# Moving a 2 KB input load from the ScalarE queue to the SyncE queue, behind the first weight load, in a one-core decode kernel

## The chip, the cores and the metric

The kernel runs on one core of one Trainium2 chip. The metric is the device time of one execution in microseconds (us). A profiled execution also gives a span, from its first to its last instruction, which is about 1.3 us shorter than the time. Kernels are compared only within the same rounds.

Names used below: PE is TensorE, DVE is VectorE, ACT is ScalarE, POOL is GpSimd, SP is SyncE. "SPq" and "ACTq" are the instruction sequencers of SP and ACT when they issue a DMA. There are 16 DMA engines; each works off packets from queues: q1 holds what SP issues, q10 what ACT issues.

## The reference, cut to what matters

One token (x of 1024 values) goes through a layer norm and then two branches that are added: a grouped-query attention over a cache of 65,536 positions with 4 key/value heads, and a small MLP block.

```python
x = A_x                                        # 1 x 1 x 1024, bf16: 2 KB
xn = _layernorm(x)
# attention: q = xn @ wq (8 MB); scores with k_cache (64 MB); softmax; times v_cache (64 MB); @ wo (8 MB)
# MLP: two layers of 1024 x 1024 (2 MB each), w3 1024 x 3584 and w4 3584 x 1024 (7 MB each)
return x + _A_ref(xn, A_k_cache, A_v_cache, A_wq, A_wo) + _B_ref(xn, B_w1, B_w2, B_w3, B_w4)
```

With one token, every byte of weights and cache is used once. About 170 MB must be read, whatever the kernel does.

## The kernel before

All large loads are issued by SP and land in one buffer with three slots of 8 MB, `KV[:, 0..2]`. Slot 0 takes wq, slot 1 takes w1 and w2, slot 2 takes w3. After that the slots take the cache blocks: K0 in slot 0, V0 in slot 1, K1 in slot 2, and so on. A slot is reloaded when the work that reads it is done.

```python
def kv_load(s, ch, src, n, bufs=None):
    _dma(q_sp, chan(ch), lambda e: e.dma_start(out=KV[:, s, 0:n], in_=src), writes=b_KV[s] if bufs is None else bufs)

_dma(q_act, chan("x"), lambda e: e.dma_start(out=x_bf, in_=A_x[0, 0, :].rearrange("(p j) -> p j", p=P)), writes=[b_x])
kv_load(0, "s0", rows_src(A_wq, 0, 8), 8 * HQD)
kv_load(1, "w1", rows_src(B_w1, 0, 8), 8 * D, b_w1)
_dma(q_sp, chan("w2"), lambda e: e.dma_start(out=KV[:, 1, 8 * D:16 * D], in_=rows_src(B_w2, 0, 8)), writes=b_w2)
kv_load(2, "s2", rows_src(B_w3, 0, 8), 8 * F)
# ... constants on POOL ...
_op(q_dve, lambda e: e.tensor_copy(xT, x_bf), reads=[b_x], writes=[b_xT])      # first DVE instruction
layer_norm(xT, b_xT, xn, xn_bf, b_xn, 200)
# ... query projection on PE: reads slot 0 and xn ...
issue(3)          # K0 into slot 0
# ... second layer norm, w1 layer, gelu, w2 layer ...
issue(4)          # V0 into slot 1
# ... third layer norm, w3 layer, gelu ...
issue(5)          # K1 into slot 2; then the cache blocks, each of which issues two more loads when it is done
```

When the program is put together, the first DMA of SP and the first of ACT are moved ahead of the start barrier, so that they go out at once. Everything else of SP's list follows the barrier.

```python
heads = {e: next(i for i in code if i.opcode == "Drain" and i.engine == e) for e in (nc.sync.engine, nc.scalar.engine)}
# ...
for eng in (nc.sync.engine, nc.scalar.engine):
    first = next(i for i in code[n_before:] if i.engine == eng)
    assert first.opcode == "DMACopy" and not first.sync_info.on_wait
    code.remove(first)
    code.insert(code.index(heads[eng]), first)
```

## Time and profile before

| | before |
|---|---|
| time, median of 3 | 400.42 us (400.32 to 400.59) |
| span of the profiled run | 399.1 us |
| data read | 169.97 MB, mean 426 GB/s |
| busy share of the span: DVE, PE, ACT | 55%, 42%, 6% |
| share of all 16 DMA engines' span taken by q1 | 98.7% |

These lines are from the profile's page of the kernel before. The first is the mean busy share of the 16 DMA engines in 40 equal slices of the span (9 is 90% or more). The two queue lines give packets, MB and the share of 16 engines' span. The last is the chain of waits that ended last, by line.

```profile
DMA  9999899999999999999999999999999999999995
...
DMA packets 3759, 169.97 MB, mean 426 GB/s; under 512 B 548, under 2 KB 552, under 8 KB 808
...
q1 hardware_dynamic: 3608, 169.87, 98.7%
...
q10 hardware_dynamic: 144, 0.00, 0.0%
...
DMA KV<-in_A_k_cache_dram 45%; DVE KV L460 18%; DMA KV<-in_B_w_dram 8%; DMA KV<-in_A_x_dram 6%; PE S_ps L411 3%; PE OT_ps L518 2%; DVE mrow L481 2%; PE M_ps L426 2%; PE S_ps L474 2%; PE S_ps L379 1%; ACT p_sb L496 1%; DVE Yall L395 1%; DVE pT_f L509 1%; DVE pT_f L419 1%; PE PT_ps L505 0%
```

The DMA engines hardly ever rest: the time seems to be set by the stream of loads. No compute engine is above 55%. Note also the 6% that the chain gives to the load of x. That figure looks like a prize of 22 us.

The next lines are from the timeline of the kernel before (those of SPq as the view of SP alone has them): start in us, duration in us, engine, line, operation, out<-in, and in brackets the idle time before it with what ended it.

```profile
0.00 0.39 SPq L290 DMA_DIRECT2D KV<-in_A_wq_dram  x1
0.12 0.37 ACTq L295 DMA_DIRECT2D KV<-in_A_x_dram  x1
...
22.24 0.17 DVE L339 CAST KV<-KV 128x8 f32<-128x8 bf16 x1 [22.24 <-DMA KV<-in_A_x_dram]
...
27.53 4.98 PE L379 MATMUL S_ps<-KV 128*32 128x512 bf16 x64 [1.36 <-DVE KV L359]
...
32.58 0.33 SPq L290 DMA_DIRECT2D KV<-in_A_k_cache_dram  x1
51.26 0.33 SPq L290 DMA_DIRECT2D KV<-in_A_v_cache_dram  x1
...
69.25 0.19 DVE L439 TENSOR_TENSOR gh_bf<-KV 128x28 bf16<-128x28 f32 x1
...
69.47 0.33 SPq L290 DMA_DIRECT2D KV<-in_A_k_cache_dram  x1
...
69.50 8.77 DVE L460 STREAM_TRANSPOSE KV<-KV 128x4096 f32<-128x4096 f32 x2
...
99.84 0.33 SPq L290 DMA_DIRECT2D KV<-in_A_v_cache_dram  x1
100.21 0.43 SPq L290 DMA_DIRECT2D KV<-in_A_k_cache_dram  x1
```

x is issued at 0.12 us and is 2 KB, yet DVE waits for it until 22.24 us. The query projection starts at 27.53 us, K0 is issued at 32.58, V0 at 51.26, K1 at 69.47 us. The first cache block (its first work is DVE L460) starts at 69.50 us, when two things are there: the output of the gelu behind w3 (DVE L439, the last work of the MLP before the cache; w4 comes at the very end), and K0, which lands at 69.48 us.

The trace's packet records show why x is late. On each engine they alternate (the records do not name the engine; a share is put together from packets that start as another ends): a 65,536 B packet of wq from q1 (2.418 us), a 16 B packet of x from q10 (0.009 us), eight times over. The Trainium skill's page "DMA: Bandwidth & Descriptors", section "Queues, rings and completion order", describes this round-robin between queue rows at packet granularity, and this trace agrees: x's packets start 2.42 us apart from 4.1 to 21.6 us. The turn here is per packet and not per byte, so the small load ends with the large one.

### The profile page before, as it was taken

To read this page: it belongs to the slowest core of one execution; us is meant where nothing else is said; L and a number is where in the kernel's file an instruction comes from. 1 tells how busy PE (TensorE), PEld (TensorE's weight loads), DVE (VectorE), ACT (ScalarE), POOL (GpSimd) and SP (SyncE) were. 2 spreads that over 40 slices of the span, in tenths; PEclk is the share of its full clock that TensorE was granted. 3 is DMA by queue.
4 is the path that set the end of the run, shared out by engine and by line. 5 is a ranking of instruction groups with operands and counts; after the bars stand their busy time and mean duration, and the time that the engine had idled before them with its cause. 6 is when DMAs were issued, how large, how long until landed. Compare 5 with 4: busy or idle time off the path is not lost.

```text
span 399.1 us, 3429 instructions
## 1 busy us (share of the span) xinstructions
PE 168.9 (42%) x1523; PEld 59.0 (15%) x1484; DVE 221.4 (55%) x260; ACT 23.9 (6%) x50; POOL 7.7 (2%) x31
## 2 busy tenths in 40 slices
PE   0034767338033713460357036413541362137394
PEld 0011334012001210110012001101120110012232
DVE  0024222994298549833984597269647952895201
ACT  1000000011001100110011002000100110011000
POOL 5000000000000000000000000000000000000000
PEclk9998568555655665575557555855585558555969
DMA  9999899999999999999999999999999999999995
GB/s 420 420 388 493 383 441 466 447 415 427 420 427 429 434 460 434 434 427 420 434 427 420 466 440 434 421 420 434 427 427 466 434 440 420 420 427 434 418 414 229
DMA packets 3759, 169.97 MB, mean 426 GB/s; under 512 B 548, under 2 KB 552, under 8 KB 808
## 3 DMA queue, kind: packets, MB, share of 16 engines
q1 hardware_dynamic: 3608, 169.87, 98.7%
q8 instruction: 5, 0.08, 0.1%
q10 hardware_dynamic: 144, 0.00, 0.0%
q14 instruction: 2, 0.02, 0.0%
HBM read 169.87 MB, written 0.00 MB: 426 GB/s over the span
## 4 chain that ended last, share of the span: by engine, by line
DMA 59%; DVE 25%; PE 12%; issue 1%; ACT 1%; SPq 1%; POOL 0%
DMA KV<-in_A_k_cache_dram 45%; DVE KV L460 18%; DMA KV<-in_B_w_dram 8%; DMA KV<-in_A_x_dram 6%; PE S_ps L411 3%; PE OT_ps L518 2%; DVE mrow L481 2%; PE M_ps L426 2%; PE S_ps L474 2%; PE S_ps L379 1%; ACT p_sb L496 1%; DVE Yall L395 1%; DVE pT_f L509 1%; DVE pT_f L419 1%; PE PT_ps L505 0%
## 5 line engine op out<-in xcount | busy, mean ns | idle before, releaser
L460 DVE STREAM_TRANSPOSE KV<-KV 128x4096 f32<-128x4096 f32 x32 | 140.3, 4422 | 44.3 <-DMA KV<-in_A_k_cache_dram 44.3
L474 PE MATMUL S_ps<-KV,Ycur 128*32 128x512 bf16 x512 | 60.7, 624 | 132.5 <-DVE KV L460 132.5
L518 PE MATMUL OT_ps<-KV,pT_f 128*32 128x512 bf16 x512 | 47.2, 511 | 4.0 <-issue 3.0
L474 PEld LDWEIGHTS S_ps<-KV,Ycur 128*32 128x32 bf16 x512 | 14.3, 126 | 160.0 <-DVE KV L460 142.4
L496 ACT ACTIVATE p_sb<-S_ps,brun 128x1024 bf16<-128x1024 f32 x16 | 17.8, 1114 | 276.6 <-DVE brun L494 176.1
L509 DVE STREAM_TRANSPOSE pT_f<-PT_ps 128x512 f32<-128x512 f32 x32 | 22.5, 702 | 14.0 <-PE PT_ps L505 14.0
L481 DVE TENSOR_REDUCE mrow<-S_ps 128x1 f32<-128x1024 f32 x16 | 19.3, 1205 | 11.3 <-PE S_ps L474 11.3
L484 PE MATMUL M_ps<-Rm,Lmat 128*128 128x16 bf16 x16 | 3.1, 194 | 38.0 <-DVE Rm L482 38.0
L529 DVE SCALAR_TENSOR_TENSOR O_acc<-O_acc,ff,OT_ps 128x512 f32<-128x512 f32 x12 | 9.0, 748 | 14.7 <-PE OT_ps L518 14.7
L518 PEld LDWEIGHTS OT_ps<-KV,pT_f 128*32 128x32 bf16 x512 | 13.1, 115 | 23.8 <-issue 16.4
L411 PE MATMUL S_ps<-KV 128*32 128x512 bf16 x88 | 12.1, 538 | 2.7 <-DVE KV L359 2.7
L339 DVE CAST KV<-KV 128x8 f32<-128x8 bf16 x1 | 0.2, 172 | 22.2 <-DMA KV<-in_A_x_dram 22.2
L578 PE MATMUL S_ps<-KV,o_bf 128*1 128x512 bf16 x64 | 9.9, 484 | 4.5 <-DMA KV<-in_A_wo_dram 4.5
L505 PE MATMUL PT_ps<-p_sb,permR 128*128 128x512 bf16 x16 | 9.7, 607 | 0.8
L426 PE MATMUL M_ps<-ident_f,pT_f 64*128 64x2 f32 (+2 forms) x32 | 7.9, 373 | 2.5 <-DVE pT_f L419 2.5
L484 PEld LDWEIGHTS M_ps<-Rm,Lmat 128*128 128x128 bf16 x16 | 1.7, 104 | 49.3 <-DVE Rm L482 49.3
L582 DVE COPY pT_f<-S_ps 1x512 f32<-1x512 f32 x1 | 0.7, 679 | 14.4 <-PE S_ps L578 14.4
L426 PEld LDWEIGHTS M_ps<-ident_f,pT_f 64*128 64x128 f32 (+2 forms) x32 | 7.7, 326 | 4.7 <-DVE pT_f L419 3.1
L419 DVE COPY pT_f<-S_ps 64x512 f32<-64x512 f32 (+1 forms) x3 | 2.1, 685 | 10.8 <-PE S_ps L411 10.8
L505 PEld LDWEIGHTS PT_ps<-p_sb,permR 128*128 128x128 bf16 x32 | 3.3, 102 | 27.5 <-ACT p_sb L496 14.7
L364 PE MATMUL M_ps<-KV 8*128 8x8 bf16 x1 | 0.2, 184 | 16.1 <-DVE Dmat_f L363 16.1
L642 POOL MEMSET pT_f<- 64x512 f32 x1 | 0.5, 520 | 312.4 <-PE OT_ps L518 312.4
(88 smaller groups left out, 90.2 us busy)
## 6 DMA issues: line engine op xcount, KB each, us to landing
KV<-in_B_w_dram SPq DMA_DIRECT2D x1, 7168.0 KB, 48.0
KV<-in_B_w_dram SPq DMA_DIRECT2D x1, 4352.0 KB, 27.4
KV<-in_B_w_dram SPq DMA_DIRECT2D x2, 2048.0 KB, 28.3
KV<-in_B_w_dram SPq DMA_DIRECT2D x1, 1792.0 KB, 31.3
KV<-in_B_w_dram SPq DMA_DIRECT2D x1, 768.0 KB, 32.7
KV<-in_B_w_dram SPq DMA_DIRECT2D x1, 256.0 KB, 32.9
KV<-in_A_k_cache_dram SPq DMA_DIRECT2D x8, 46.7
KV<-in_A_v_cache_dram SPq DMA_DIRECT2D x8, 28.1
```

What stands on the lines that cost most here:

```text
L411: fns.append(lambda e, j=j, k=k, mv=mv: e.matmul(S_ps[32 * (k % 4):32 * (k % 4) + 32, bank + k // 4, :], vec[:, j:j + 1].broadcast_to([P, ...
L419: _op(q_dve, lambda e, b=b, nb=nb: e.tensor_copy(pT_f[0:32 * nb, b, :], S_ps[0:32 * nb, bank + b, :]), reads=[b_S[bank + b]], writes=[b_pT ...
L426: fns.append(lambda e, b=b, nb=nb, c=c: e.matmul(M_ps[:, c0 + 16 * b + c:c0 + 16 * b + 4 * nb:4], pT_f[0:32 * nb, b, c:512:4], ident_f[0:3 ...
L460: _op(q_dve, lambda e: e.transpose(out=KV32[:, s, o:o + 4096], in_=KV32[:, s, o:o + 4096]), reads=[b_KV[s][sub]], writes=[b_KV[s][sub]], l ...
L474: fns.append(lambda e, we=we, cm=cm, mv=mv: e.matmul(S_ps[32 * cm:32 * cm + 32, n % 4, :], Ycur[:, we, :, :].rearrange("p a g -> p (a g)") ...
L481: _op(q_dve, lambda e: e.reduce_max(mrow[:, k:k + 1], S_ps[:, 2 * k:2 * k + 2, :].rearrange("p b c -> p (b c)"), axis=AX.X), reads=b_S[2 * ...
L496: _op(q_act, lambda e: e.activation(p_sb[:, :, :].rearrange("p b c -> p (b c)"), S_ps[:, 2 * k:2 * k + 2, :].rearrange("p b c -> p (b c)") ...
L505: _op(q_pe, lambda e: e.matmul(PT_ps[:, :], permR[:, :], p_sb[:, n % 2, :], start=True, stop=True), reads=[b_p[n % 2], b_const], writes=[b ...
L509: _op(q_dve, lambda e: e.transpose(out=pT_f[:, n % 2, :], in_=PT_ps[:, :]), reads=[b_PT], writes=[b_pT[n % 2]], loop=True)
L518: fns.append(lambda e, q=q, q4=q4: e.matmul(OT_ps[32 * q4:32 * q4 + 32, g % 2, :], pT_bf[:, n % 2, q, :, 1], KV[:, s, 8192 * sub + 512 * q ...
L529: _op(q_dve, lambda e: e.scalar_tensor_tensor(out=O_acc[:, 0:512], in0=O_acc[:, 0:512], scalar=ff[:, k:k + 1], in1=OT_ps[:, k, :], op0=ALU ...
L578: _grp(q_pe, [lambda e, j=j, jj=jj: e.matmul(S_ps[32 * jj:32 * jj + 1, 1, :], o_bf[:, j:j + 1], KV[:, 0, j * D + 512 * jj:j * D + 512 * (j ...
```

## The change

The load of x is issued by SP, directly behind wq. ACT has no DMA any more, so only SP's first DMA (wq) is moved ahead of the barrier. One may hope that ACT's start is relieved, that wq no longer shares its engines with x, and that x arrives as wq does, in time for the projection that needs both.

```diff
-        _dma(q_act, chan("x"), lambda e: e.dma_start(out=x_bf, in_=A_x[0, 0, :].rearrange("(p j) -> p j", p=P)), writes=[b_x])
         kv_load(0, "s0", rows_src(A_wq, 0, 8), 8 * HQD)
+        _dma(q_sp, chan("x"), lambda e: e.dma_start(out=x_bf, in_=A_x[0, 0, :].rearrange("(p j) -> p j", p=P)), writes=[b_x])
...
-        heads = {... for e in (nc.sync.engine, nc.scalar.engine)}
+        heads = {... for e in (nc.sync.engine,)}
...
-        for eng in (nc.sync.engine, nc.scalar.engine):
+        for eng in (nc.sync.engine,):
```

## The prediction

> **What bounds the kernel.** The stream of weight and cache loads on the SyncE queue. The profile's page gives 169.97 MB at a mean of 426 GB/s; SyncE's queue (q1) takes 98.7% of all 16 DMA engines' span. The trace's packet records show 64 KB packets back to back at 2.418 us each (16 x 65,536 B / 2.418 us = 434 GB/s). Unused engine time sums to about 5.4 us: 1.2 us before the first packets, 3.9 us in the last 10 us, only about 0.25 us between. So only what delays or lengthens this stream moves the time.
>
> **What x does now.** The ScalarE queue issues x at 0.12 us, yet the timeline's first DVE instruction (the cast of x) waits until 22.24 us, for x. x is only 2 KB; it is late because of sharing. In the packet records each engine alternates: one 65,536 B packet of wq on q1, one 16 B packet of x on q10, eight times, from 4.1 to 21.6 us. The Trainium skill ("DMA: Bandwidth & Descriptors", section "Queues, rings and completion order") describes this round-robin by packet; the trace agrees. x's last completion is at 22.21 us, wq's at 22.02 us. Issuing x from another queue thus buys no early x.
>
> **What the change removes, adds, moves.** It takes a 0.37 us DMA issue from ScalarE's start and adds about 0.4 us to SyncE's, between wq and w1. w1 goes out near 1.3 us in place of 0.92 us: harmless, wq keeps the engines until 21 us. x's eight 16 B packets and its completion now stand behind wq's eight packets in the same ring. Each takes 0.009 us in the records, so about 0.08 us per engine, the same work in another place. wq should finish about 0.07 us earlier, x at about 22.1 to 22.5 us.
>
> **How much is critical.** The chain x, layer norm, query projection (27.53 to 32.58 us) frees slot 0, and the first K load is issued at 32.58 us. But it queues behind w1, w2 and w3, which occupy the engines until about 48 us: some 15 us of slack. The V load is issued at 51.26 us, while K keeps the engines until 67 us; the next K load at 69.47 us, with V keeping them until 86 us. A shift of x by a few us is swallowed. The end (w4, last rows, output) only follows the stream. The chain of waits lists the x load with 5.5%, but in those 22 us the wq load is needed by the same projection and lands at the same time, so that share cannot be won.
>
> **Predicted:** 400.4 us, range 399.7 to 401.1 us; faster by over 2%: 0.01; within 2%: 0.975; slower by over 2%: 0.015.
>
> **What would show it right.** q10 disappears and q1 gains 144 packets; the cast of x still waits for x until 22.0 to 22.6 us; x's packets stand in a cluster near 21 us; the query projection starts within 0.5 us of 27.53 us; the first K load lands as before (67 to 69.5 us); the last w4 landing (396.6 us) moves by under 0.5 us.
>
> **What would make it wrong.** Nine tiny packets in a row in one ring leave a bubble that alternating with big ones hid (each waits a memory round trip, not 9 ns): everything behind shifts one to a few us later, up to 1%. Or x's issue blocks SyncE so long that w1 is late (needs over 18 us). Or the stream starts sooner without ScalarE's request beside it (the first wq packets take about 3.1 us in place of 2.42): gain of some tenths.

## The result, and the profile after

The changed kernel takes 400.53 us (median of 6 runs, 400.35 to 400.83); the kernel before in the same rounds 400.50 us (400.32 to 400.77). The ratio is 1.0001, with a 95% interval of 0.9988 to 1.0014: the same. Ratios here are the mean time of one kernel's fast runs over that of the other's of the same rounds, so they are not quite the ratio of the medians quoted.

From the page of the changed kernel, the queue line:

```profile
q1 hardware_dynamic: 3752, 169.88, 98.7%
```

q10 is gone, and q1 has its 144 packets (3608 + 144 = 3752). The stream's share is the same to the digit.

The timeline of the changed kernel, the same events as before:

```profile
0.00 0.39 SPq L290 DMA_DIRECT2D KV<-in_A_wq_dram  x1
0.80 0.33 SPq L296 DMA_DIRECT2D KV<-in_A_x_dram  x1
1.18 0.42 SPq L290 DMA_DIRECT2D KV<-in_B_w_dram  x1
...
22.16 0.17 DVE L339 CAST KV<-KV 128x8 f32<-128x8 bf16 x1 [22.16 <-DMA KV<-in_A_x_dram]
...
27.45 5.68 PE L379 MATMUL S_ps<-KV 128*32 128x512 bf16 x64 [1.36 <-DVE KV L359]
...
33.19 0.33 SPq L290 DMA_DIRECT2D KV<-in_A_k_cache_dram  x1
...
70.02 0.19 DVE L439 TENSOR_TENSOR gh_bf<-KV 128x28 bf16<-128x28 f32 x1
...
70.22 13.09 DVE L460 STREAM_TRANSPOSE KV<-KV 128x4096 f32<-128x4096 f32 x3
...
99.63 0.33 SPq L290 DMA_DIRECT2D KV<-in_A_v_cache_dram  x1
```

x is issued 0.68 us later and is used 0.08 us earlier. It is now late for a different reason: not because its packets take turns with wq's, but because they stand behind them. The packet records of one engine's share at the seam look like this (start in us, queue, duration in us, bytes; the 4 B packets are completions):

```
after 20.933 q1 0.009 4        <- wq's completion
after 20.939 q1 0.009 16       <- x, eight runs of 16 B
after 20.945 q1 0.009 16
...
after 20.981 q1 0.009 16
after 20.986 q1 0.009 4        <- x's completion
after 20.992 q1 0.611 16384    <- w1
```

The x load occupies this engine for 0.053 us (20.992 less 20.939), and w1 follows without a bubble.

One difference is visible: the projection took 5.68 us where it took 4.98, and K0 was issued 0.6 us later. In both traces the matmuls start 0.107 us apart on average at first and 0.054 us apart later; the change of pace comes at 30.3 us before and 31.6 us after, with nearly the same start of the projection. The trace's record of the granted clock begins at just these moments (30.30 and 31.61 us, full clock), and all its stretches but the last, which the end of the trace cuts, are multiples of 3.41 us long. The Trainium skill's page "TensorE: Matmul & The Clock Gate", section "What's actually happening", says that the PE clock is released by a free-running activity window of about 3.4 us, so that the moment varies with its phase. This agrees with the factor of two in pace and with the differing moment, which in the eleven profiled kernels came 2.8 to 5.7 us after the start of the projection. The 0.6 us ended nowhere: V1 was issued at 99.63 us, even a little earlier than before.

### The profile page after: what moved, and what is told of

Its sections match the earlier page's. It is cut to its first block, busy times and chain, and to the rows that moved or that the text cites. A ratio compares the mean times of both kernels' runs of the same rounds, so it can differ in the third digit from the quotient of the medians.

```text
span 399.2 us, 3429 instructions
## 1 busy us (share of the span) xinstructions
PE 169.1 (42%) x1523; PEld 59.1 (15%) x1484; DVE 221.3 (55%) x260; ACT 23.9 (6%) x50; POOL 7.7 (2%) x31
## 3 DMA queue, kind: packets, MB, share of 16 engines
q1 hardware_dynamic: 3752, 169.88, 98.7%
## 4 chain that ended last, share of the span: by engine, by line
DMA 58%; DVE 25%; PE 13%; issue 1%; ACT 1%; SPq 1%; POOL 0%
DMA KV<-in_A_k_cache_dram 45%; DVE KV L460 17%; DMA KV<-in_B_w_dram 8%; DMA KV<-in_A_x_dram 5%; PE S_ps L411 3%; PE OT_ps L518 2%; DVE mrow L481 2%; PE M_ps L426 2%; PE S_ps L474 2%; PE S_ps L379 1%; ACT p_sb L496 1%; DVE Yall L395 1%; DVE pT_f L509 1%; DVE pT_f L419 1%; PE PT_ps L505 0%
## 5 line engine op out<-in xcount | busy, mean ns | idle before, releaser
L578 PE MATMUL S_ps<-KV,o_bf 128*1 128x512 bf16 x64 | 8.8, 443 | 4.5 <-DMA KV<-in_A_wo_dram 4.5
```

The source lines that it names most:

```text
L578: _grp(q_pe, [lambda e, j=j, jj=jj: e.matmul(S_ps[32 * jj:32 * jj + 1, 1, :], o_bf[:, j:j + 1], KV[:, 0, j * D + 512 * jj:j * D + 512 * (j ...
```

## The experiments

The theory: the load stream sets the time; x only has to arrive soon enough that the next loads are issued before the engines run dry; and whether it comes by turns or in line makes no difference to that. The main rival takes the chain of waits at its word: x's load is 5 to 6% of the critical path, and the change moved nothing only because x came equally late both times. (By this rival an early x is worth some 5 us and not 22, as the projection would still wait for wq until about 22 us.) Two more questions were open: how much lateness is really swallowed, and whether tiny packets in a row in one queue cost more than their 6 ns. The nine kernels below all gave the right result.

| kernel | cast of x starts | MLP done | V1 issued | median | minus before, same rounds |
|---|---|---|---|---|---|
| x first on SP | 1.65 | 66.39 | 99.83 | 401.09 | +0.58 |
| x on ACT, wq in four | 8.05 | 65.68 | 98.90 | 400.60 | +0.09 |
| before | 22.24 | 69.25 | 99.84 | 400.50 | |
| after | 22.16 | 70.02 | 99.63 | 400.53 | +0.03 |
| x in the middle of w1 | 24.61 | 73.53 | 103.39 | 400.75 | +0.30 |
| x behind w1 | 27.09 | 75.80 | 105.55 | 402.24 | +1.73 |
| x behind w2 | 31.81 | 79.80 | 109.43 | 405.71 | +5.20 |
| x behind w3 | 48.78 | 96.00 | 125.47 | 421.48 | +21.06 |

All in us; the first three columns of figures come from one trace each, the last is the difference of two medians. "MLP done" is the start of the last instruction of the second gelu, the one behind w3 (DVE L439 above; L440 where the edit adds a line).

### x early, without touching the stream: x on ACT, wq in four loads

```diff
 # on the kernel before: x stays on ACT
-        kv_load(0, "s0", rows_src(A_wq, 0, 8), 8 * HQD)
+        for i in range(4):
+            _dma(q_sp, chan("wq%d" % i), lambda e, i=i: e.dma_start(out=KV[:, 0, 2 * i * HQD:2 * (i + 1) * HQD], in_=rows_src(A_wq, 2 * i, 2)), writes=[b_KV[0][i]])
```

> The kernel before (x on the ScalarE queue), with wq loaded as four DMAs of two rows, so that its packets are 16 KB and not 64 KB. Theory (the load stream binds; x is late only because each of its 16 B packets waits its turn behind one big packet): x's packets now alternate with 0.61 us packets, so x lands at about 6 to 7.5 us in place of 22.2; the query projection starts when wq lands, near 22.2 us in place of 27.5, the first K load is issued near 28 us in place of 32.6 to 33.2; the total stays at 400.5 us within 0.6. Rival 1 (the chain of waits is right that the x load is 5% of the critical path): about 5 us faster, 395 us. Rival 2 (x is late because the descriptors of the first request on the other queue must drain first): x still lands at about 22 us.

Measured: 400.60 us, ratio 1.0001 (0.9986 to 1.0016). From its timeline:

```profile
8.05 0.17 DVE L340 CAST KV<-KV 128x8 f32<-128x8 bf16 x1 [8.05 <-DMA KV<-in_A_x_dram]
...
22.26 6.24 PE L380 MATMUL S_ps<-KV 128*32 128x512 bf16 x64 [10.28 <-DMA KV<-in_A_wq_dram]
...
28.55 0.33 SPq L290 DMA_DIRECT2D KV<-in_A_k_cache_dram  x1
...
65.68 0.19 DVE L440 TENSOR_TENSOR gh_bf<-KV 128x28 bf16<-128x28 f32 x1
...
69.38 13.10 DVE L461 STREAM_TRANSPOSE KV<-KV 128x4096 f32<-128x4096 f32 x3 [3.41 <-DMA KV<-in_A_k_cache_dram]
```

The same bytes in packets a quarter as long bring x 14 us sooner (half a microsecond past the expected 7.5), its packets now some 0.6 us apart. That is the round-robin by packet, shown by changing the packet. (The landing alone would not tell it from a rule that x waits for the first load on the other queue, as the first quarter of wq lands at 7.14 us; that the packets of x come one by one, 0.6 us apart from 2.8 to 6.9 us, does.) The projection now waits for wq and starts 5.3 us sooner, and K0 is issued 4.0 us sooner. All of that is lost again: the MLP is done 3.6 us sooner, but the first cache block then waits for K0, which comes with the stream, and starts at 69.38 us as it did before (69.50). The time does not move. The rival's 5 us are not there.

### x first on SP

```diff
 # on the changed kernel
+        _dma(q_sp, chan("x"), ...)          # unchanged, only moved up
         kv_load(0, "s0", rows_src(A_wq, 0, 8), 8 * HQD)
-        _dma(q_sp, chan("x"), ...)
```

x is now SP's first DMA, so it takes wq's place ahead of the start barrier.

> x on the SyncE queue ahead of wq; x is now the DMA that is issued before the start barrier, wq the one after it. Theory: x lands near 2.5 to 3 us and the query projection starts near 23 us (when wq lands), but wq's first packet starts 0.8 us later (1.8 in place of 1.0 us), and a late start of the stream is never made up: 401.2 us, +0.5 to +1.0. Rival (x is critical): 5 us faster less 0.8, about 396 us.

Measured with five rounds: 401.09 us (400.96 to 401.26) against 400.51 (400.37 to 400.83); ratio 1.0012, 95% interval 0.9999 to 1.0026. From its timeline:

```profile
0.00 0.39 SPq L295 DMA_DIRECT2D KV<-in_A_x_dram  x1
...
0.80 0.33 SPq L290 DMA_DIRECT2D KV<-in_A_wq_dram  x1
...
1.65 0.67 DVE L339 CAST KV<-KV 128x8 f32<-128x8 bf16 x1 [1.65 <-DMA KV<-in_A_x_dram]
...
22.85 6.37 PE L379 MATMUL S_ps<-KV 128*32 128x512 bf16 x64 [12.17 <-DMA KV<-in_A_wq_dram]
...
70.39 13.10 DVE L460 STREAM_TRANSPOSE KV<-KV 128x4096 f32<-128x4096 f32 x3 [3.70 <-DMA KV<-in_A_k_cache_dram]
```

With nothing ahead of it, x is there 1.65 us after its issue began (2.5 to 3 were expected); all the rest of the usual 22 us was queueing. Having it 20 us sooner gains nothing: again the first cache block waits for K0. And the wq load that went out 0.80 us later seems to cost what it delays: wq's first packet starts at 1.76 us in place of 1.01, the last w4 load lands at 397.29 us in place of 396.68, and the median is 0.58 us up. The interval of the ratio only just includes 1, so take the size from the trace and the medians together rather than from the ratio alone.

### Lengthening the stream: one more MB

```diff
 # on the changed kernel; before V0 is issued, SP also waits for this load
         kv_load(2, "s2", rows_src(B_w3, 0, 8), 8 * F)
+        _dma(q_sp, chan("xc"), lambda e: e.dma_start(out=KV[:, 1, 16 * D:20 * D], in_=rows_src(B_w1, 0, 4)))
```

> The changed kernel with 1 MB more loaded behind w3 (four rows of w1 again, to unused columns). Theory (stream-bound): 1,048,576 B at 434 GB/s is 2.42 us more, 402.9 us. Rival (something else binds, the stream has slack): 400.5 us.

Measured: 402.92 us against 400.42, +2.50 us; ratio 1.0062 (1.0045 to 1.0079). Added bytes cost their full time. Together with the two runs above: moving x by 14 or 20 us is worth nothing, 2.4 us of extra stream are worth 2.5 us.

### x late: behind w1, behind w2, behind w3

```diff
 # on the changed kernel: the load of x moved down by one, two or three loads
         kv_load(0, "s0", rows_src(A_wq, 0, 8), 8 * HQD)
-        _dma(q_sp, chan("x"), ...)
         kv_load(1, "w1", rows_src(B_w1, 0, 8), 8 * D, b_w1)
+        _dma(q_sp, chan("x"), ...)                            # behind w1
         _dma(q_sp, chan("w2"), ...)                           # or behind w2
         kv_load(2, "s2", rows_src(B_w3, 0, 8), 8 * F)         # or behind w3
```

> x behind w1 on the SyncE queue: x lands near 26.9 us, 4.8 us later than in the changed kernel. Theory: swallowed, 400.5 us within 0.6; V1 and K2 are issued near 104.4 us in place of 99.6, just before the engines run dry at 105.8. Rival (x is critical): +4.8 us, 405.3 us.

> x behind w2: x lands near 31.9 us, 9.8 us later. By the slack that the prediction gave (some 15 us until the engines run dry at 48 us, and again at 67 and 86) this is swallowed: 400.5 us. By the trace of the changed kernel the tightest slack is another: the first cache block starts when the MLP is done (70.2 us), takes 29.4 us, and only then are V1 and K2 issued (99.6 us), while the engines have K1 until 105.8 to 107.8. Then the slack is about 6 us, V1 is issued near 109.4 us, the engines stand idle for 3 to 4.5 us, and the total is about 404.3 us. If x were critical throughout: 410 us.

> x behind w3: x lands near 49.9 us, 27.8 us later. By the 15 us slack alone: about 412 us (one stall of 12 to 13 us before K0). By the second slack too (V1 issued near 127 us): another stall of 8 to 9 us, 421 to 423 us in all. If x were critical throughout: 428 us.

Measured: behind w1 402.24 us (ratio 1.0047, interval 1.0032 to 1.0062), behind w2 405.71 us (1.0132, 1.0117 to 1.0148), behind w3 421.48 us (two runs; 1.0526, 1.0504 to 1.0547).

The stretch from 100 to 112 us, where V1 and K2 should follow K1, tells the story. These are lines of the view by stretches; the columns are the stretch, its length, then busy us of PE, PEld, DVE, ACT and POOL, the granted clock, the share of the 16 DMA engines that was busy (it can pass 1 in a short stretch, as packets are counted where they fall) and GB/s. First the changed kernel:

```profile
100.00:112.00 12.00, 0.00 (x0) 0.00 (x0) 4.37 (x3) 0.00 (x0) 0.00 (x0) 0.64 1.01 437
```

x behind w1:

```profile
100.00:112.00 12.00, 5.22 (x58) 1.33 (x50) 6.88 (x7) 0.88 (x3) 0.00 (x0) 0.78 0.89 366
```

x behind w2:

```profile
100.00:112.00 12.00, 8.10 (x80) 2.13 (x72) 6.97 (x13) 1.29 (x3) 0.00 (x0) 0.74 0.68 273
```

x behind w3, with the stretch in which K0 should follow w3 as well:

```profile
44.00:62.00 18.00, 7.23 (x82) 2.77 (x51) 4.28 (x20) 0.60 (x1) 0.56 (x1) 1.00 0.29 109
...
112.00:124.00 12.00, 8.64 (x77) 2.13 (x69) 8.20 (x12) 1.61 (x5) 0.00 (x0) 0.58 0.51 218
```

(The clock of 1.00 in the first of these two lines is no reading: that trace's clock record starts at 57.31 us, and the view prints 1.00 where there is none.)

When V1 was issued is in the timelines; x behind w1, then x behind w2:

```profile
105.55 0.33 SPq L290 DMA_DIRECT2D KV<-in_A_v_cache_dram  x1
```

```profile
109.43 0.33 SPq L290 DMA_DIRECT2D KV<-in_A_v_cache_dram  x1
```

K1's first completions arrive at 106.3 us in the changed kernel. With x behind w2, V1 goes out 3 us after that time, and the packet records show the engines unused for 4.4 us (mean of the 16) between 105 and 115 us. Nothing of the kind is seen at 48 us or at 67 us, where the prediction had looked for the slack. With x behind w3 there are two such holes, 12.6 us between w3 and K0 and 7.1 us between K1 and V1 (12 to 13 and 8 to 9 expected). A stream that ran dry also started slowly again: V1's first 16 packets took 2.94 us on average behind w1 and 3.06 us behind w2, in place of 2.42. In the profile behind w2 the 4.4 us unused and the 0.6 us of slow packets make up the whole loss (span 404.3 us, 5.05 us longer than the changed kernel's). So the theory of a single slack of 15 us (400.5 and 412 us) fell, and so did "x is critical throughout" (410 and 428 us). The account with the second slack, read from the changed kernel's trace (404.3, and 421 to 423 us), was nearly right: 1.4 us too low behind w2, and right behind w3. Behind w1 it had said "swallowed", with V1 issued at 104.4 us, and 1.7 us were lost, with V1 issued at 105.55 us. There the matmuls' slow pace lasted some 5.3 us into the projection (it took 6.24 us in all), so the MLP was done 5.8 us later than in the changed kernel for an x that came 4.9 us later. The four runs spread over 1.3 us, against 0.5 us for the kernel before. The profiled one was the fastest of them, 1.0 us over the changed kernel in its span, of which 0.5 us are unused engines and 0.5 us slow packets. Whether the phase of the clock window makes the spread is not shown: one run of the four has a trace.

### A little late: x between the halves of w1

```diff
-        kv_load(1, "w1", rows_src(B_w1, 0, 8), 8 * D, b_w1)
+        _dma(q_sp, chan("w1"), lambda e: e.dma_start(out=KV[:, 1, 0:4 * D], in_=rows_src(B_w1, 0, 4)), writes=[b_KV[1][0]])
+        _dma(q_sp, chan("x"), ...)                            # in place of behind wq
+        _dma(q_sp, chan("w1b"), lambda e: e.dma_start(out=KV[:, 1, 4 * D:8 * D], in_=rows_src(B_w1, 4, 4)), writes=[b_KV[1][1]])
```

> w1 in two halves with x between them: x lands near 24.6 us, 2.4 us later than in the changed kernel. If the slack is 3 to 5 us, as the runs with x behind w1 (4.9 us later, +1.7 us) and behind w2 (9.7 us later, +5.2 us) suggest, this costs nothing: 400.5 us within 0.6, and V1 is issued near 102 to 103 us. If every us of lateness costs its share from the first on (a third of it, as behind w1): 401.3 us.

Measured: 400.75 us, ratio 1.0006 (0.9989 to 1.0022). V1 was issued at 103.39 us, a little past the expected 102 to 103, and the engines stay full but for 0.1 us:

```profile
103.39 0.33 SPq L290 DMA_DIRECT2D KV<-in_A_v_cache_dram  x1
```

```profile
100.00:112.00 12.00, 3.16 (x45) 0.88 (x37) 5.89 (x6) 0.00 (x0) 0.00 (x0) 0.78 1.01 431
```

An x that is 2.4 us late is swallowed within the error of the runs. By the losses behind w1 and w2 (1.7 us for 4.9 us of lateness, 5.2 for 9.7), the changed kernel has some 3 to 4.5 us of slack for x, not 15.

### Tiny packets: 64 more loads of x, one by one, and in one DMA

```diff
 # on the changed kernel, behind w3, to unused columns; before V0 is issued, SP waits for them
+        for i in range(64):
+            _dma(q_sp, chan("xc"), lambda e, i=i: e.dma_start(out=KV[:, 1, 16 * D + 8 * i:16 * D + 8 * i + 8], in_=A_x[0, 0, :].rearrange("(p j) -> p j", p=P)))
```

> The changed kernel with 64 more loads of x (2 KB each, to unused columns) behind w3 on the SyncE queue: 576 more packets on each engine. In the changed kernel x's nine packets followed each other at 0.0058 us. Theory (what is added to the stream lengthens the run in full; a tiny packet costs some 6 ns): 64 x 9 x 0.0058 = 3.3 us more, 403.9 us. Rival (tiny packets in a row in one ring wait for a memory round trip each DMA[...], hidden in the changed kernel by something else): 30 us more. If small packets cost nothing: 400.5 us.

Measured: 427.43 us, +27.0 us: near the rival's figure, but for another reason, so it doesn't count for the rival. The timeline:

```profile
2.72 70.72 SPq L303 DMA_DIRECT2D KV<-in_A_x_dram  x64
73.49 0.43 SPq L290 DMA_DIRECT2D KV<-in_A_k_cache_dram  x1
```

SP issued nine DMAs in 4.7 us (wq, x, w1, w2, w3 and four of the copies); the tenth issue then took 14.36 us, as if it could not get rid of its work. Once the stream had drained, near 48 us, the rest went out 0.474 us apart, so K0 came only at 73.49 us. The run measured the issue of DMAs and not their packets. It failed at what it was made for; the next one asks for the packets alone, with a single issue.

```diff
+        _dma(q_sp, chan("xc"), lambda e: e.dma_start(out=KV[:, 1, 16 * D:16 * D + 512].rearrange("p (r j) -> p r j", j=8),
+                 in_=A_x[0, 0, :].rearrange("(p j) -> p j", p=P).unsqueeze(1).broadcast_to([P, 64, 8])))
```

> The changed kernel with one more DMA behind w3 that reads x 64 times into unused columns: 8192 runs of 16 B, 512 tiny packets per engine and one completion, from a single issue. The 64 separate issues of the run before were limited by the issues themselves (0.47 us from one to the next once the queue had drained), so that run said nothing of the packets. Theory (a tiny packet costs the engine the 0.0058 us at which x's packets followed each other): 512 x 0.0058 = 3.0 us more, 403.5 us. Rival (tiny packets cost a round trip that the few of one x load hide): far more, 10 us or over. Limit from the other side (descriptors are made more slowly than the engines take them): between the two, with idle gaps of a steady length between the tiny packets.

Measured: 419.07 us (418.12 to 420.13), +18.6 us, ratio 1.0472 (1.0448 to 1.0497). In the packet records the tiny packets go fast for the first half microsecond or so (478 of them from 48.0 to 48.5 us) and then settle at about 212 in each half microsecond until 55.5 us and again from 58 to 62.5 us, with a second burst in between (660 from 56.5 to 57.0 us). Nearly all are still recorded at 7 to 9 ns. Each engine had 512 of them; the first engine was done at 57.8 us and the last at 67.6 us, so from 47.8 us on that is 19 to 39 ns for each. SP again could not get rid of its next DMA:

```profile
33.37 28.51 SPq L290 DMA_DIRECT2D KV<-in_A_k_cache_dram  x1
```

So "a tiny packet costs 6 ns" is wrong for long rows of them, and right for the nine of one x load. The first burst, the steady rate and the blocked issue fit the third account (descriptors are made more slowly than the engines take them), but the second burst is not explained by it, and no run here measured the making of descriptors by itself; whether it is that or a limit of the engines stays open. For the change at hand it doesn't matter: its nine packets were measured directly, 0.053 us on an engine.

## Why the prediction was right, and where its reasoning was not

- **The bound.** Right. The stream binds: one more MB cost 2.50 us for 2.42 expected.
- **x gains nothing by being on its own queue, and loses nothing behind wq.** Right. The cast of x moved from 22.24 to 22.16 us (range given: 22.0 to 22.6), the projection from 27.53 to 27.45, the last w4 landing from 396.56 to 396.68, all within what was said.
- **"That share cannot be won."** Right. Two kernels took the x wait away; the projection then waited for wq until 22.3 or 22.9 us, and the time stayed or rose by 0.6 us.
- **"Each takes 0.009 us, so about 0.08 us per engine."** Slightly too large: the packets start 0.0058 us apart, and the whole x load took 0.053 us.
- **"Some 15 us of slack", "a shift of x by a few us is swallowed".** This step failed, though the change never tested it. The slack was looked for at K0, V0 and K1, where it is indeed 14 to 17 us. It was not followed one step further: the first cache block starts when the MLP is done (70.2 us), takes 29.4 us, and only its end frees the slots for V1 and K2 (99.6 us), while K1's first completions come at 106.3 us. That leaves 6 to 7 us less the start of a DMA (1.0 us from issue to first packet at the kernel's start), and the runs lost 1.7 us for 4.9 us of lateness and 5.2 us for 9.7. Part of the gap is in the traces: behind w1 the MLP came 5.8 us later for an x that came 4.9 later, and the restarted stream cost 0.5 to 0.6 us in slow first packets.
- **The three ways to be wrong.** None came about for this change. Nine tiny packets left no bubble; a slower pace was seen only in long rows of them. SP's issue of x took 0.33 us and w1 went out at 1.18 us. The start without ACT's request was not sooner: the first wq packets took 2.98 us on average in place of 3.13, but started up to 0.3 us later, and unused engine time before the stream was full was 1.4 us in place of 1.2.

No version here beats the two kernels. The stream itself has little left to take: the packet records of the kernel before leave about 5.4 us of engine time unused in 399 us, nearly all of it at the start and the end.

## What to carry to other kernels

In a chain of waits, the share of a load that lands together with a larger load needed by the same instruction is no prize; look at what the instruction would wait for next, and then whether anything downstream reaches the resource that binds. The small load beside a large one waited one large packet for each of its own small packets here; where such a load is really needed early, try issuing it first, or cutting the large one up (1.65 and 8.05 us here in place of 22.24), and look whether the time moves. When you claim slack, follow the delay through every later point where it decides when a load is issued, and take the smallest; here it was at the end of the first cache block, 30 us after the last of the places where it looked comfortable.

## What the Trainium skill lacked or had wrong

- "DMA: Bandwidth & Descriptors", section "Queues, rings and completion order", gives the round-robin by packet, with 9 to 17 descriptors as a typical packet. Here every contiguous run was a packet of its own, 65,536 B or 16 B, so that a 2 KB load took 22 us beside 64 KB packets, 8 us beside 16 KB packets and 1.65 us with nothing ahead of it. The page does not draw this consequence for small loads beside large ones.
- The same page's advice that DMAs from several issuing engines run on the same 16 DMA engines and interleave (section "Issuing engines are not separate DMA queues") holds here: x's packets from ACT took turns with wq's from SP, and the time was 400.50 us with x on ACT and 400.53 us with x on SP. What I found in none of its sections on issuing is how many DMAs one queue takes before the issuing sequencer stalls: on SP the tenth issue took 14.36 us with nine DMAs ahead of it, and a DMA behind one of 8192 tiny runs took 28.51 us to issue.
- The same page's section "Bandwidth" derives about 10.5 ns a packet from small GpSimd-issued DMAs. Issued from SP, nine small packets (eight of 16 B and the completion) followed each other at 5.8 ns on one engine, but 512 in a row took 19 to 39 ns each. The section does not say whether its figure is for one engine, so the two may not be like for like.
- The same section says that for loads from HBM the HBM side (about 358 GB/s) binds; with one core running, this kernel's packets moved 434 GB/s (16 x 65,536 B in 2.418 us), close to the fabric ceiling of 435 GB/s that the page also gives. The section itself says that its own measurement of 425 GB/s was made with the other core of the pair idle; the sentence on 358 GB/s lacks that condition.
